# Loading and turning one tile of u earlier, and moving another load of u to a later hook, in a fused gated attention and feed-forward kernel

## The chip, the cores and the metric

The kernel runs on one core of a Trainium2 chip. The metric is the device time of one execution in microseconds (us). Times inside a profile are counted from the first instruction of the span.

## The reference

There are 8 batches of 3072 rows. `u` and `v` have 256 columns, `z` has 64. Attention is made from `z` alone, so the score matrix is symmetric, and there is no softmax:

```python
scores = scale * np.matmul(z, z.transpose(0, 2, 1))   # scale = 1 / 3072
attn = np.maximum(scores, 0.0) ** 2
x = u * np.matmul(attn, v)                            # 24576 rows of 256
h1, h2 = x @ w1, x @ w2                               # 256 -> 1024
out = np.maximum(h1, h2) @ w_out                      # 1024 -> 256
```

All inputs and the output are 32-bit floats.

## The kernel before

**Tiles.** The rows of a batch are 24 tiles of 128. Four tiles are a group (`G = 4`, 6 groups per batch), two groups a couple (3 per batch). The score matrix of a batch is handled in 4x4-tile blocks, `A[b, g, blk]`, kept in 28 slots of SBUF (class `Block`). Only blocks with `blk >= g` are computed; a block on the other side of the diagonal is the transpose of its partner, made by a DMA transpose from SBUF to SBUF (`mirror`, L273, the DMA issued at L275). A score pair (`score_pair`, L209) is two matmuls (L223) into two PSUM tiles `s_ps`, a ReLU on ScalarE (L236) and a square on VectorE (L244).

**Stages.** Groups 0 to 3 of batch 0 are done one by one (loop `for i in range(PLAIN)`, L617). For each, `attn_unit` (L286) multiplies the blocks with `v` into four accumulators, and the code between the matmuls issues scores ahead, loads, transposes and the gates. Here `i` is the group, `n` the tile of the step. The edges of a group run all its tiles for one half of the columns (`dc = 0`) and then for the other; what is hooked to a tile `n` is issued in the pass with `dc = 0`. After that come the couples, from couple 2 of batch 0 on (L758), each a list of steps of two matmuls each (L908). Couple 2 of batch 0 is a "plain" one (`PLAIN_COUPLES`, L46): it needs no sums of blocks prepared, and it works through the blocks 4 and 5 first (steps 0 to 31), then 0 and 1, then 2 and 3. All later couples form seven products from sums of blocks (a Strassen scheme). Before each couple stands a feed-forward stage for two earlier groups (`second`, L705, which calls `ff`, L448, twice). The first such stage, for groups 0 and 1 of batch 0, is the one at L753.

**u.** `load_u` (L189) allocates a tile `un` from a pool of two buffers and loads it by GpSimd-issued DMAs (L195), in two DMAs for groups above 1. With `held=True` a one-column memset on VectorE (L192) goes first, so that the DMA waits for the place of that memset in VectorE's order. `turn_u` (L197) transposes it by a DMA that SyncE issues (L199) into a tile `uT`, also from a pool of two. The gate (`gate`, L433; instruction L437 on VectorE, one per half of the columns) multiplies the attention result with `uT` into `xT`, the input of the feed-forward. With two buffers, the load of `u` of group 5 takes the buffer of group 3, and may start when the turn of group 3 has read it.

**Feed-forward.** `ff` first makes 8 tiles `d_ps` (L453) with a ReLU on ScalarE (L460) each, then two PSUM tiles `o_ps` (L467, L476) of two 128-row tiles each. A ScalarE copy (L488) moves each into a tile `o_sb` from a pool of three buffers, and a DMA on GpSimd's queue (L489) writes it out. `hook(1, nb)` is called after each of the 8 parts, `hook(2, t)` after the matmuls of row tile `t` and before the copy and the output that follow an odd `t`. `second` puts its list of tasks, one at a time, at the hooks (1, 0), (1, 3), (2, 0), (2, 1), (2, 2), (2, 3) of each `ff`:

```python
places = {(1, 0): 1, (1, 3): 1, (2, 0): 1, (2, 1): 1, (2, 2): 1, (2, 3): 1}
...
for _ in range(places.get((stage, n), 0)):
    if tasks:
        tasks.pop(0)()
```

The tasks come from `prepared` (L726), which for a plain couple returns the gates alone:

```python
if i in PLAIN_COUPLES:
    return {}, list(gates)
```

**z.** The transposed `z` of a batch is in three pieces of eight tiles, turned by `turn_z` (L147, DMA at L151 on SyncE's queue). Pieces of batch 1 are turned during group 2 (piece 0) and group 3 (pieces 1 and 2) of batch 0, since couple 2 of batch 0 computes scores of batch 1 between its steps. Its first scores on piece 1 stand at step 27, those on piece 2 at step 61.

**Order.** The program is laid out by hand (`tc.manual_schedule()`): each engine runs its instructions in the order in which the code issues them, and waits on semaphores where an instruction needs another engine's or a DMA's result, or a buffer that is still in use. SyncE's queue carries all DMA transposes (mirrors, u, z, and once w2, L673); GpSimd's queue carries the loads of u, v, z and the outputs. Around the change SyncE's order is: turn of u of group 2, transpose of w2, mirror (0,4), z piece 0, mirror (1,4) at tile 20 of group 2, mirrors (3,4) and (0,5) at tile 0 of group 3, turn of u of group 3 at tile 3, mirror (1,5), z piece 1, mirror (3,5), z piece 2, then the turns of u of groups 4 and 5. Mirror (g, blk) is the block of rows g and columns blk.

Of the kernel before, what the change touches and what calls it, by code (L numbers as in the profile page):

```python
# [11 lines left out]
def kernel(  # L12
# [55 lines left out]
    def by_tile(x):  # L68
        return x.rearrange("(p t) d -> p t d", t=NT)
# [34 lines left out]
    def load(tile_, source):  # L104
        dma = nc.gpsimd.dma_start(out=tile_, in_=source)  # L105
        if pace:
            tc.add_manual_dep(dma.ins, pace[-1].ins.name, AFTER, reason="paced")
# [23 lines left out]
    def zT_pe(lo, n, engine):  # L131
        tp = mm_psum.tile([P, n, P], bf16, name="tpz", tag="mm")
        for j in range(n):
            nc.tensor.transpose(
                tp[:, j, :], zd_first(lo + j, 1).rearrange("p t h d -> p (t h d)"), ident
            )
        copy = nc.scalar.copy if engine == "act" else nc.vector.tensor_copy
        for k in range(0, n, G):
            copy(zT[:, lo + k : lo + k + G, :], tp[:, k : k + G, :])
# [49 lines left out]
    def load_u(b, g, held=False):  # L189
        un[b, g] = unat.tile([P, G, D], bf16, name="un")  # L190
        if held:
            nc.vector.memset(un[b, g][:, 0, 0:1], 0.0)  # L192
        step = 2 if b or g > 1 else G
        for k in range(0, G, step):
            load(un[b, g][:, ds(k, step), :], by_tile(u[b])[:, ds(g * G + k, step), :])  # L195

    def turn_u(b, g):  # L197
        t = upool.tile([P, G, KD, P], bf16, name="uT")
        nc.sync.dma_start_transpose(  # L199
            t.rearrange("p a c r -> p (a c) r"), un[b, g].rearrange("p a d -> p (a d)")  # L200
        )
        uT[b, g] = t
# [70 lines left out]
    def mirror(b, g, blk):  # L273
        t = Block(turned=True)
        nc.sync.dma_start_transpose(  # L275
            t.ap.rearrange("p (k r) -> p k r", r=P), A[b, g, blk].ap
        )
        A[b, blk, g] = t
        A[b, g, blk].release(after=COOL)
# [6 lines left out]
    def attn_unit(b, g, t, acc, dc, first, last):  # L286
        blk, j = divmod(t, G)
        a = A[b, g, blk]
        for half in range(2):
            rows = ds(half * R, R)  # L290
            nc.tensor.matmul(  # L291
                a.out(acc[half, dc]),
                v_at(b, t, dc)[rows],
                a.moving(rows, j),
                start=first,
                stop=last,
            )
        if dc == KD - 1 and j == G - 1:
            a.release()
# [4 lines left out]
    def drain(acc, dcs, copy=nc.scalar.copy):  # L304
        hs = {}
        for dc in dcs:
            hs[dc] = new_h()
            copy(hs[dc], acc[1, dc])
        for dc in dcs:
            nc.vector.tensor_add(hs[dc], hs[dc], acc[0, dc])  # L310
        return hs

    def drain_fast(acc, dc):
        hs = [new_h() for half in range(2)]
        nc.scalar.copy(hs[1], acc[1, dc])
        nc.vector.tensor_copy(hs[0], acc[0, dc])
        return hs
# [205 lines left out]
    def emit_pair(wait=0):  # L523
        nonlocal done
        early = done < 12
        finish = score_pair(
            *pairs[done], dve_half=1 if early and done % 3 == 0 else None, halves=done == 0
        )
        done += 1
        if wait:  # L530
            due.append((tick + wait, finish))
        else:
            finish()
# [10 lines left out]
    def steps_of(i):  # L544
        tiles, both = range(NT), range(KD)
        head = edge(i - 1) if i else 0
        tail = NT - edge(i)
        steps = [(n, dc) for dc in both for n in tiles[:head]]
        steps += [(n, dc) for n in tiles[head:tail] for dc in both]
        return steps + [(n, dc) for dc in both for n in tiles[tail:]]  # L550

    def pair_slots(i):
        return (
            [1, 3] + list(range(6, 40, 4)),
            list(range(3, 41, 4)),
            list(range(3, 41, 4)),
            list(range(0, 44, 4)),
        )[i]

    def need(b, g, n):  # L560
        most = pair_at[b, g, 2 * g]
        for t in range(n + 1):
            if t // G >= g:
                most = max(most, pair_at[b, g, t // 2] + 1)
        return most

    with tc.manual_schedule():
# [18 lines left out]
        def new_acc():  # L586
            return {
                (half, dc): acc_tile(2 * half + dc) for half in range(2) for dc in range(KD)
            }
# [27 lines left out]
        for i in range(PLAIN):  # L617
            b, g = groups[i]
            if i:
                acc = new_acc()  # L620
            new, slots = {}, pair_slots(i)
            for slot, (n, dc) in enumerate(steps_of(i)):
                tick += 1
                k = need(b, g, n)
                upto = max(k, min(done + 1, k + AHEAD)) if slot in slots else k
                while done < min(upto, len(pairs)):
                    emit_pair()
                if i == 0 and slot in (10, 22):
                    zT_pe(12 if slot == 10 else 20, 8 if slot == 10 else 4, "act")
                    if slot == 22:  # L630
                        for x in z_first:
                            x.release()
                attn_unit(b, g, n, acc, dc, n == 0, n == NT - 1)
                if n == NT - 1 and i < PLAIN - 1:
                    if i < 2:
                        new[dc] = drain_fast(acc, dc)
                    else:
                        new.update(drain(acc, [dc]))
                if dc:
                    continue  # L640
                if i in (1, 2) and n in (5, 8):
                    k = n // 8
                    nc.vector.tensor_add(sums[k][0], *sums[k])
                    sums[k] = sums[k][0]
                first = 17 if i == 3 else 11
                if i and n == first:
                    gates = gate(*groups[i - 1], sums)
                if i and n in (first, first + 3):
                    gates.pop(0)()
                if i == 0 and n == 14:  # L650
                    turn_u(0, 0)
                if (i, n) in ((1, 8), (2, 1), (3, 1)):
                    load_u(0, i, held=True)
                if (i, n) == (3, 14):
                    load_u(0, 4, held=True)
                if i and n == (0, 16, 14, 3)[i]:
                    turn_u(0, i)
                if (i, n) in ((0, 18), (2, 12)):
                    w_in = ((w2_sb, moe_w2), (w1_sb, moe_w1)) if i == 0 else ((w_out_sb, moe_w_out),)
                    nc.vector.memset(w_in[0][0][:, 0, 0:1], 0.0)  # L660
                    for w_sb, w in w_in:
                        nc.gpsimd.dma_start(
                            out=w_sb, in_=w.rearrange("(c p) f -> p c f", p=P)
                        )
                if later and n % 4 == 0 and (i == 3 or i and n > 12):
                    later.sort(key=lambda block: block[2])
                    mirror(*later.pop(0))
                if i == 2 and n == 16:
                    nc.vector.tensor_sub(w15_sb, w1_sb, w2_sb)
                    w1.release()  # L670
                    w2.release(after=COOL)
                if (i, n) == (2, 15):
                    nc.sync.dma_start_transpose(  # L673
                        w2T.ap.rearrange("p (k r) -> p k r", r=P), w2.ap
                    )
                if (i, n) in ((1, 16), (2, 14)):
                    load_z(1, i - 1, held=True)
                if (i, n) in ((2, 17), (3, 4)):
                    turn_z(1, i - 2)
                if (i, n) == (3, 5):  # L680
                    load_z(1, 2, held=True)
                if (i, n) == (3, 17):
                    turn_z(1, 2)
            sums = new
# [41 lines left out]
        def prepared(i, gates):  # L726
# [25 lines left out]
        forms, tasks = prepared(PLAIN // 2, gate(b, g, sums))  # L752
        second(  # L753
            PLAIN // 2 - 2,
            [lambda: load_u(0, 5)] + tasks,
        )

        for i in range(PLAIN // 2, len(couples)):  # L758
# [177 lines left out]
            if i + 1 < len(couples):  # L936
                forms, tasks = prepared(i + 1, gates)
            else:
                tasks = gates
# [33 lines left out]
```

## Time and profile before

| | |
|---|---|
| median of 5 runs | 919.12 us (915.37 to 919.2) |
| the profiled execution | 918.5 us |
| its span, first to last instruction | 916.7 us |
| mean granted clock of TensorE | 0.996 |
| TensorE busy | 899.2 us, 98% of the span |
| VectorE busy | 722.3 us, 79% |
| ScalarE busy | 601.4 us, 66% |
| GpSimd busy | 161.0 us, 18% |
| DMA moved | 145.61 MB, mean 159 GB/s |

In the profile, PE is TensorE (PEld its weight loads), DVE is VectorE, ACT is ScalarE, POOL is GpSimd and SP is SyncE. A row of a timeline gives start, duration (both in us), engine, line of the kernel, instruction, output<-input and the number of instructions merged into the row; in brackets follow the idle time of the engine before it and what ended that. A q behind an engine's name stands for its instruction queue. A row of a table by stretches gives the stretch, its length, the busy time and number of instructions of each engine (TensorE, its weight loads, VectorE, ScalarE, GpSimd), the granted share of TensorE's clock, the mean busy share of the DMA engines (with overlaps counted, so it can pass 1), and GB/s. A row of the chain gives start, duration and what the end of the program was waiting for.

### The profile page before, as it was taken

The page shows a single profiled execution, that of the slowest core. Times are in us where ns is not written, and L with a number is a line of the kernel's source. Part 1 is how long each engine was busy: PE and PEld are TensorE (multiplying, and loading weights), DVE is VectorE, ACT ScalarE, POOL GpSimd, SP SyncE. Part 2 cuts the span into 40 slices and gives each one's busy share as a digit, 9 for nine tenths or more (in the row PEclk, how much of TensorE's full clock was granted, in tenths as well). Part 3 has the DMA queues.
Part 4 walks back from the last instruction along what each step waited for, and adds up shares of the span by engine and source line. Part 5 has one row for each costly group of instructions (what it writes and reads, how often), then busy time and mean ns, then how long its engine had stood idle before and what let it go on. Part 6 is the DMA issues. An engine that isn't in the chain of part 4 may idle for free.

```text
span 916.7 us, 19395 instructions
## 1 busy us (share of the span) xinstructions
PE 899.2 (98%) x7478; PEld 520.1 (57%) x7526; DVE 722.3 (79%) x1098; ACT 601.4 (66%) x1192; POOL 161.0 (18%) x303
## 2 busy tenths in 40 slices
PE   9996999999999999999999999999999999999998
PEld 4454465564655655656556656466465564655655
DVE  6743599788997799987998979979799788995640
ACT  7973966667676676666766676766666667673445
POOL 4111111212202122111212021130230212101000
PEclk9998999999999999999999999999999999999999
DMA  9999998999999897999969999799989989988201
GB/s 175 176 163 194 177 166 132 197 176 155 180 174 162 176 165 151 178 154 169 202 114 204 148 173 169 136 204 159 157 171 142 186 162 171 160 160 145 78 24 70
DMA packets 396557, 145.61 MB, mean 159 GB/s; under 512 B 361904, under 2 KB 387632, under 8 KB 396464
## 3 DMA queue, kind: packets, MB, share of 16 engines
q1 hardware_dynamic: 359040, 91.79, 65.0%
q0 software_dynamic: 37424, 52.58, 32.0%
q8 instruction: 59, 0.97, 0.5%
q14 instruction: 34, 0.28, 0.1%
HBM read 59.77 MB, written 25.17 MB: 93 GB/s over the span
## 4 chain that ended last, share of the span: by engine, by line
PE 94%; DMA 3%; DVE 1%; issue 1%; ACT 1%; SPq 0%; POOL 0%; ACTq 0%; POOLq 0%; DVEq 0%
PE acc L908 44%; PE o_ps L476 18%; PE d_ps L453 18%; PE s_ps L223 7%; PE o_ps L467 4%; PE acc L291 2%; DMA blk<-blk 1%; DMA out_dram<-o_sb 1%; ACT r_sb L236 1%; DMA un<-in_u_dram 1%; DVE blk L244 1%; DMA uT<-un 0%; PE acc L595 0%; PE w2o_ps L691 0%; SPq L275 0%
## 5 line engine op out<-in xcount | busy, mean ns | idle before, releaser
L908 PE MATMUL acc<-blk,v_sb 64*128 64x512 bf16 x2208 | 453.5, 378 | 0.0
L236 ACT ACTIVATE r_sb<-s_ps 128x512 bf16<-128x512 f32 (+3 forms) x672 | 335.4, 559 | 120.3 <-PE s_ps L223 76.1
L908 PE MATMUL acc<-blk,vt 64*128 64x512 bf16 x1512 | 364.1, 376 | 0.0
L908 PEld LDWEIGHTS <-v_sb 64*128 64x128 bf16 x2208 | 179.3, 94 | 142.4 <-issue 15.4
L244 DVE TENSOR_TENSOR blk<-r_sb 128x1024 bf16<-128x1024 bf16 x257 | 172.4, 688 | 88.2 <-ACT r_sb L236 82.7
L460 ACT ACTIVATE g_sb<-d_ps 128x512 bf16<-128x512 f32 x384 | 193.4, 626 | 29.4 <-PE acc L908 17.9
L476 PE MATMUL o_ps<-w_out_sb,g_sb 128*128 128x256 bf16 x1536 | 175.5, 273 | 0.0
L908 PEld LDWEIGHTS <-vt 64*128 64x128 bf16 x1512 | 139.2, 94 | 62.9
L453 PE MATMUL d_ps<-xT,w_sb 128*128 128x512 bf16 x720 | 167.7, 379 | 2.6 <-issue 0.2
L476 PEld LDWEIGHTS <-g_sb 128*128 128x128 bf16 x1536 | 150.3, 98 | 17.3
L488 ACT COPY o_sb<-o_ps 128x512 f32<-128x512 f32 (+1 forms) x98 | 56.4, 578 | 141.3 <-PE o_ps L476 131.7
L223 PE MATMUL s_ps<-zT 64*128 64x512 bf16 (+3 forms) x676 | 131.4, 358 | 7.7 <-ACT o_sb L488 7.4
L489 POOL DMA_DIRECT2D out_dram<-o_sb x88 | 48.2, 548 | 498.6 <-ACT o_sb L488 498.6
L785 DVE TENSOR_TENSOR h_sb<-h_sb,acc 128x512 f32<-128x512 f32 x168 | 109.4, 682 | 28.3 <-ACT h_sb L789 20.9
L453 PEld LDWEIGHTS <-w_sb 128*128 128x128 bf16 x768 | 73.3, 98 | 89.4 <-issue 9.8
L347 DVE TENSOR_TENSOR blk<-blk,blk 128x2048 bf16<-128x2048 bf16 x63 | 77.2, 1225 | 4.5 <-DMA blk<-blk 2.4
L343 DVE TENSOR_TENSOR blk<-blk,blk 128x2048 bf16<-128x2048 bf16 x63 | 76.7, 1218 | 0.0
L800 DVE TENSOR_TENSOR blk<-blk,blk 128x2048 bf16<-128x2048 bf16 x63 | 76.6, 1218 | 0.0
L351 DVE TENSOR_TENSOR blk<-blk,blk 128x2048 bf16<-128x2048 bf16 x63 | 73.3, 1219 | 3.3 <-DMA blk<-blk 3.3
L105 POOL DMA_DIRECT2D un<-in_u_dram x94 | 50.2, 549 | 124.5 <-DMA uT<-un 87.6
L437 DVE SCALAR_TENSOR_TENSOR xT<-h_sb,uT 128x512 bf16<-128x512 f32 x96 | 62.0, 684 | 6.3 <-DMA uT<-un 5.0
L242 DVE TENSOR_TENSOR blk<-r_sb 128x512 bf16<-128x512 bf16 (+3 forms) x162 | 46.2, 323 | 19.5 <-ACT r_sb L236 18.5
(49 smaller groups left out, 357.9 us busy)
## 6 DMA issues: line engine op xcount, KB each, us to landing
out_dram<-o_sb POOLq DMA_DIRECT2D x88, 256.0 KB, 3.8
un<-in_u_dram POOLq DMA_DIRECT2D x92, 128.0 KB, 5.2
v_sb<-in_v_dram POOLq DMA_DIRECT2D x74, 128.0 KB, 6.0
blk<-blk SPq DMA_TRANSPOSE x240, 5.0
v_sb<-in_v_dram POOLq DMA_DIRECT2D x11, 256.0 KB, 7.3
zn<-in_z_dram POOLq DMA_DIRECT2D x21, 128.0 KB, 4.7
out_dram<-o_sb SPq DMA_DIRECT2D x6, 256.0 KB, 2.0
blk<-in_moe_w_dram POOLq DMA_DIRECT2D x2, 512.0 KB, 7.6
```

The source lines that it names most:

```text
L223: nc.tensor.matmul(s_ps[h][:, lo[h] :], zT[rows, z_at(b, blk * G + tiles[h]), :], zT[rows, q + lo[h] // P : q + G, :].rearrange("p t c -> ...
L236: nc.scalar.activation(o, s, AF.Relu)
L244: nc.vector.tensor_mul(a[:, k : k + 2, :], r, r)
L343: nc.vector.tensor_add(*alike(f["S1"], f["A21"], f["A22"]))
L347: nc.vector.tensor_sub(*alike(f["S2"], f["S1"], f["A11"]))
L351: nc.vector.tensor_sub(*alike(f["S3"], f["A11"], f["A21"]))
L453: nc.tensor.matmul(d_ps, w15_sb[:, kc, ts(nb, P)], xT[:, kc, :], start=(kc == 0), stop=(kc == KD - 1),)
L460: nc.scalar.activation(g_sb[:, nb, :], d_ps, AF.Relu)
L476: nc.tensor.matmul(o_ps[t // 2][:, t % 2, :], g_sb[:, nb, ts(t, P)], w_out_sb[:, nb, :], start=False, stop=(nb == KF - 1 and t % 2 == 1),)
L785: nc.vector.tensor_add(out, a, b_)
L800: nc.vector.tensor_sub(f["A12"].ap, f["A12"].ap, f["S2"].ap)
L908: mm = nc.tensor.matmul(a.out(acc[name]), w()[rows], a.moving(rows, j), start=name not in opened, stop=left[name] == 0,)
```

## The change

`u` of group 3 was loaded at tile 1 of group 3 and turned at its tile 3. It is now loaded at tile 19 of group 2 (`i + n // 19` is 3 there) and turned at tile 22 of group 2. In the first feed-forward stage, the load of `u` of group 5 was the first of the tasks that the stage takes at its hooks; it is now put behind the first three tasks of the list, or behind all of them where there are fewer.

```diff
-                if (i, n) in ((1, 8), (2, 1), (3, 1)):
-                    load_u(0, i, held=True)
+                if (i, n) in ((1, 8), (2, 1), (2, 19)):
+                    load_u(0, i + n // 19, held=True)
                 if (i, n) == (3, 14):
                     load_u(0, 4, held=True)
-                if i and n == (0, 16, 14, 3)[i]:
+                if (i, n) == (2, 22):
+                    turn_u(0, 3)
+                if (i, n) in ((1, 16), (2, 14)):
                     turn_u(0, i)
...
         forms, tasks = prepared(PLAIN // 2, gate(b, g, sums))
         second(
             PLAIN // 2 - 2,
-            [lambda: load_u(0, 5)] + tasks,
+            tasks[:3] + [lambda: load_u(0, 5)] + tasks[3:],
         )
```

## The prediction, made before the changed kernel ran

> **What bounds the kernel now.** I first read busy shares and the slices: TensorE is busy 899.2 of 916.7 us, so only a TensorE hole can pay. The change touches u of groups 3 and 5, so I asked for the chain that ended last around the first ff stage (start, length, what; us):
>
> ```profile
> 71.94 3.42 PE d_ps L453 x15
> 75.36 1.54 SPq L275
> ...
> 77.06 3.25 DMA uT<-un
> ...
> 81.38 0.52 POOL un L105
> 81.91 6.25 DMA out_dram<-o_sb
> ...
> 88.26 0.59 ACT o_sb L488
> ```
>
> Here the chain leaves TensorE: turned u of group 3 lands at 77.06+3.25 = 80.31, then GpSimd loads u of group 5, then the first output goes out and lands at 88.16, then ScalarE copies. The timeline of TensorE gives the hole, and the stretches after it the clock:
>
> ```profile
> 81.16 0.38 PE L223 MATMUL s_ps<-zT 64*128 64x512 bf16 x1
> 88.89 0.58 PE L223 MATMUL s_ps<-zT 64*128 64x512 bf16 x1 [7.36 <-ACT o_sb L488]
> 88.90 2.28 PE L908 MATMUL acc<-blk,v_sb 64*128 64x512 bf16 x8
> 84.00:88.00 4.00, 0.00 (x0) 0.00 (x0) 0.00 (x0) 0.00 (x0) 0.00 (x0) 0.74 1.22 257
> 88.00:92.00 4.00, 3.10 (x16) 1.35 (x17) 1.39 (x2) 3.30 (x7) 0.55 (x1) 0.50 1.28 173
> ```
>
> TensorE stands 7.36 us, for ScalarE's copy of the fourth o_sb; pool o_sb has three buffers, so that copy waits for output 1 to land. The granted clock then is 0.50. It falls at 85.92 and is full again at 92.75, so 92.75 - 88.89 = 3.86 us of matmuls run at half speed and lose 1.93. The hole costs 7.36 + 1.93 = **9.29 us**. GpSimd's timeline says why output 1 was late:
>
> ```profile
> 63.74 1.06 POOL L105 DMA_DIRECT2D un<-in_u_dram  x2 [8.66 <-DVE un L192]
> 80.86 1.06 POOL L105 DMA_DIRECT2D un<-in_u_dram  x2 [16.06 <-DMA uT<-un]
> 81.91 1.64 POOL L489 DMA_DIRECT2D out_dram<-o_sb  x3
> ```
>
> Three outputs leave at once behind the load of u of group 5, although ScalarE had copied the first at 70.77. That load needs the buffer of u of group 3, so it waits 16.06 us for the turn. The turn is late because SyncE's queue runs far behind the code (the x3 issue at 66.71, 70.86 and 72.96):
>
> ```profile
> 64.92 1.68 SPq L151 DMA_TRANSPOSE zT<-zd  x1
> 66.71 10.18 SPq L275 DMA_TRANSPOSE blk<-blk  x3
> 77.06 1.23 SPq L199 DMA_TRANSPOSE uT<-un  x1
> 78.39 1.71 SPq L275 DMA_TRANSPOSE blk<-blk  x1
> 80.20 1.89 SPq L151 DMA_TRANSPOSE zT<-zd  x1
> ```
>
> [...] transposes move about 1000 packets per us alone (77 to 79), some 300 while loads and outputs run (82 to 91).
>
> **Part 1: u of group 3 earlier.** Load: one 59 ns VectorE memset and two GpSimd DMAs (0.53 us each) move from tile 1 of group 3 to tile 19 of group 2, from 50.56 to about 47.5. They stay behind the same z load and ahead of the next, so no queue order on GpSimd changes. The z load ahead of them lands at 53.65 and their packets come after its, so I count no gain and no loss. Were the zn load slowed by 1 us, VectorE's copies (waiting 2.17 us for it) would be 1 us later; pools r_sb and s_ps cover that, uncovered 1 us. The buffer is free (the turn of group 1 landed at 37.37), so the memset waits for nothing; it comes before L310, whose wait costs TensorE 0.44 us at 48.49: at most 0.06 more.
>
> Turn: one SyncE instruction of 1.23 us. Following the code, the line of mirrors there is (1,4) at 66.71 (tile 20 of group 2), (3,4) at 70.86, (0,5) at 72.96 (both tile 0 of group 3). The turn moves from behind (0,5) to behind (1,4), past two mirrors. It issues at 70.8 instead of 77.06, 6.3 us earlier; its inputs landed long before and its target is free since the gate of group 1 at 45.1. Mirror (1,4) lands at 72.62; 1024 packets more at about 800 per us, the rate there, is 1.3: **landing about 73.9** (it was 1.30 behind its predecessor in the trace too). Late bound: an instruction fetch of 1.6 us at 74.72 held transposes until 77.1; a turn caught by it lands near 77.
>
> **Part 2: u of group 5.** The list of tasks for this ff stage holds only the two gates of group 3, since couple 2 is a plain one and nothing else is prepared. So tasks[:3] is both gates, and the load becomes task three, run at the hook after tile t=0 of the o_ps part. The first output is written at t=1. **The load is thus still ahead of the first output on GpSimd's queue**; only the gates move up one place on VectorE, where nothing stands between. They run after the L310 adds end at 75.44 instead of 80.43, and nothing waits for them. Part 2 costs and brings 0.
>
> **What is late next.** GpSimd: landing 73.9, loads 0.55 later at 74.45, output 1 at 73.9 + 1.60 = 75.5 (offsets as in the trace: 80.31, 80.86, 81.91). Output 1 takes 6.25 us, as before behind the same two loads: lands at 81.75. The same fetch may hold it; I add 0.5, half of a delay of about 1 us. TensorE is unhurt when the copy starts by 80.8 (0.7 us from landing to matmul, needed at 81.4). So a hole of 82.25 - 80.75 = **1.5 us** stays (bounds 0, if the output lands in 5 us, and 4)[...].
>
> Next comes z. The scores of step 27 of couple 2 (TensorE at 96.19) need z transpose piece 1, issued at 80.20 and landed at 86.58: 9.6 us of slack. TensorE now comes there 9.29 - 1.5 = 7.8 earlier, at 88.4. SyncE's total up to that issue is the same, being a permutation, but loads and outputs now fall on 75 to 82 instead of 82 to 88 and take bandwidth from mirrors (0,5), (1,5) and this z. About 3000 packets fewer in that stretch are 3 us, of which the outputs' earlier end gives back about half: landing near 88 +/- 2. Mean hole **0.6 us** (bounds 0 and 3). Mirrors (0,5) and (1,5) are in front of it in the queue and needed only from step 32, at 89.5. Mirror (3,5), landing 92.38 before, is needed from step 68, near 99. The last v load landed at 118.33 for VectorE's use at 124.82; its issue is paced by TensorE, so 6.5 us of cover moves along. SyncE waits for new work at 126.19, so its backlog is gone there; from 92.75 to 881 no TensorE gap is above 0.08 us, so the shift should reach the end.
>
> **Sum.** 9.29 - 1.5 - 0.6 = 7.2 us. The profiled execution: span 916.7 to 909.5, with the 1.8 us around it 918.5 to 911.3. The median before, 919.12, is 0.6 above that execution: **911.9**.
>
> **Rivals.**
> A, the forecast: gain 5 to 8.5, time 910.6 to 914.1; chance 0.60.
> B, output 1 really escapes the wait, because it goes first or lands in under 5 us: no hole, only z to wait for, 9.29 - 0.3 = 9.0, time 910.1 (909.1 to 910.6). For: the description says outputs go first. Against: the task list is two long. 0.12.
> C, the turn is caught by the fetch or by mirrors' packets and lands at 77 or later: output at 78.6, landing 84.8, hole 4.1 with about 1 us of clock lost; gain 9.29 - 5.1 = 4.2, less 0.6 for z: 915.5 (914.1 to 916.3). For: that fetch stands 0.8 us behind the expected landing. 0.14.
> D, no difference: the wait moves whole to z piece 1, DMA being what bounds the stretch (DMA share 1.2 from 80 to 119); TensorE standing at step 27 until about 95: 918. Against: in 76 to 80 the share was 0.88, so there is room. 0.08.
> E, slower: the turn in front of mirrors (3,4) and (0,5), with outputs on their heels, delays z piece 1. Slower by 2.76 us means that after a gain of 7.8 step 27 stands 10.5 us, of which 1.9 is clock: z lands at 88.4 + 8.6 = 97.0, 10.4 later than before. At 98 the time is 922.9. The moved turn is 1.3 us of DMA time, so that needs a queue collapse that I don't see: 0.06.
>
> 0.3%, 2.76 us, is about what a measurement of this kernel can tell from no change. Faster: A + B + C = 0.86; within: D = 0.08; slower: E = 0.06. Range 909.2 to 916.0: A, nearly all of B, most of C, about 0.82. The low end is the whole 9.29 and the 0.63 wait for w2's transpose (64.74) gone too.
>
> **What would show it.** Right: GpSimd's 16.06 us wait shrinks to about 9 (64.8 to 74.45); output 1 leaves at 75 to 76, still behind both loads; the gap of 7.36 is under 2.5 and the clock stays full at 85; a small new wait for zT may stand near 88. Wrong: output ahead of the loads (B); turn landing after 77 (C); a long TensorE wait on zT or a mirror between 85 and 100 (D, E).

## The result, and the profile after

The changed kernel takes as long as the kernel before, or 0.1% longer: 918.67 us (median of 43 executions) against 917.52 us (80 executions of the kernel before on the same chips), a ratio of 1.0014 with a 95% interval of 1.0002 to 1.0025. I had forecast 911.9 us. Single executions spread from 914.0 to 928.8, those of before from 914.1 to 923.4, so one profile of either kernel is one draw. The ratios in this document leave out executions more than 1.5% above the fastest of the same kernel; where that leaves out many of them (7 of 22 in e4, 8 of 22 in e13), the median of all is given beside the ratio.

The profiled execution took 918.47 us. Its span is 915.5 us, 1.2 us shorter than before, but 3.0 us lie outside the span, where it was 1.8. The matmul of group 0 that waits for w2's memset starts 1.06 us later in it than in the profile of before (20.79 against 19.73), so times in this stretch compare after taking 1.06 off. The chain that ended last (start, duration, what; us):

```profile
71.89 3.35 DMA uT<-un
...
76.31 0.52 POOL un L105
76.84 9.18 DMA out_dram<-o_sb
86.12 0.59 ACT o_sb L488
```

The first output no longer waits for a late turn: it leaves at 76.84 instead of 81.91. But it needs 9.18 us to land, where it needed 6.25. The timelines of GpSimd and then of SyncE:

```profile
75.79 1.06 POOL L105 DMA_DIRECT2D un<-in_u_dram  x2 [10.13 <-DMA uT<-un]
76.84 1.11 POOL L489 DMA_DIRECT2D out_dram<-o_sb  x2
```

```profile
71.89 1.23 SPq L199 DMA_TRANSPOSE uT<-un  x1
73.29 13.31 SPq L275 DMA_TRANSPOSE blk<-blk  x3
86.70 1.31 SPq L151 DMA_TRANSPOSE zT<-zd  x1
```

Both loads of u of group 5 are still ahead of the first output. SyncE turns u of group 3 first, but the three mirrors behind it, (3,4), (0,5) and (1,5), take 13.31 us to issue, and z piece 1 is issued at 86.70 instead of 80.20 and lands at 91.64 instead of 86.58. TensorE's timeline, and then two stretches of time (columns as explained above):

```profile
86.75 0.58 PE L223 MATMUL s_ps<-zT 64*128 64x512 bf16 x1 [4.13 <-ACT o_sb L488]
```

```profile
84.00:88.00 4.00, 1.25 (x7) 0.49 (x8) 0.27 (x1) 1.88 (x4) 0.54 (x1) 0.72 1.10 269
88.00:92.00 4.00, 4.00 (x22) 1.75 (x20) 1.80 (x3) 2.51 (x6) 0.53 (x1) 0.50 1.18 249
```

The hole is 4.13 us long instead of 7.36. The clock is half from 85.73 to 92.56, so the restart loses (92.56 - 86.75) / 2 = 2.9 us instead of 1.93. In this draw the hole costs 7.0 us and not 9.29. Of these 2.3 us the start that is 1.06 us later takes nearly half, which leaves the 1.2 us by which the span is shorter.

### The profile page after: what moved, and what is told of

The parts are those of the page before. It is cut to its first block, busy times and chain, and to the rows that moved or that the text cites. A ratio compares the mean times of both kernels' runs of the same rounds, so it can differ in the third digit from the quotient of the medians.

```text
span 915.5 us, 19396 instructions
## 1 busy us (share of the span) xinstructions
PE 901.0 (98%) x7478; PEld 521.5 (57%) x7526; DVE 722.8 (79%) x1098; ACT 601.9 (66%) x1192; POOL 160.2 (18%) x303
## 4 chain that ended last, share of the span: by engine, by line
PE 95%; DMA 2%; ACT 1%; DVE 1%; issue 1%; SPq 0%; POOL 0%; ACTq 0%; DVEq 0%; POOLq 0%
PE acc L910 44%; PE d_ps L453 18%; PE o_ps L476 18%; PE s_ps L223 7%; PE o_ps L467 4%; PE acc L291 3%; DMA out_dram<-o_sb 1%; ACT r_sb L236 1%; DMA zT<-zd 1%; DVE blk L244 0%; DMA uT<-un 0%; PE acc L595 0%; PE tpz L134 0%; DVE w_sb L671 0%; DVE xT L437 0%
```

## The experiments

The experiments set two theories against each other: H, the loss is the hole behind the fourth output copy, and the rest of the stretch has slack; M, the DMA engines have so much to do between 60 and 130 us that a wait taken away in one place comes back in another. Each run has a label, as e2; the text in front of its result is what was expected before it ran.

### Part 2 alone (e2)

```diff
-            [lambda: load_u(0, 5)] + tasks,
+            tasks[:3] + [lambda: load_u(0, 5)] + tasks[3:],
```

> The kernel before with part 2 alone (the load of u of group 5 behind the tasks). My working says that part 2 leaves GpSimd's order as it was, so all theories expect a ratio of 1.000 +/- 0.002, GpSimd issuing both loads of u of group 5 ahead of the first output after a wait of about 16 us, and TensorE's gap of about 7 us for the fourth output copy. If part 2 did something of its own, the order of loads and outputs in the trace would differ from before. The run also gives a second profiled execution of what should be the same program as before, and so shows how much the gap varies.

Ratio 1.0007 (0.9989 to 1.0025). The instruction lists of all five engines are, in their order, those of the kernel before; those of part 1 alone are likewise those of the whole change. Part 2 does nothing. The profiled execution of what is the same program as before has a hole of 5.56 us and half speed from 82.66 to 89.49: 5.56 + (89.49 - 86.10) / 2 = 7.3 us. The 9.29 I counted was one draw of a varying loss.

### The outputs really first (e3)

```diff
-            tasks[:3] + [lambda: load_u(0, 5)] + tasks[3:],
+            tasks + [lambda: None] * 4 + [lambda: load_u(0, 5)],
```

> The changed kernel, with the load of u of group 5 put at the first hook of the second ff, so that it really stands behind outputs 1 and 2. Theory H (the loss is the hole behind the fourth output copy, the rest of the stretch has slack): outputs 1 and 2 leave at about 72 and 74, output 1 lands before 80, no gap at the fourth copy, ratio 0.990 to 0.993. Theory M (DMA work bounds the stretch, the wait only moves): a new wait of TensorE of 4 us or more on z piece 1 (step 27 of couple 2) or on a mirror between 85 and 100, ratio 0.996 to 1.001.

Ratio 1.0008 (0.9988 to 1.0029). Outputs 1 and 2 leave at 71.59 and 73.34, the first lands at 76.05, and the hole at the copy is gone. TensorE now waits for z:

```profile
91.22 0.61 PE L223 MATMUL s_ps<-zT 64*128 64x512 bf16 x2 [3.75 <-DMA zT<-zd]
```

That is M's wait, a little under the 4 us it named. H falls: with the outputs really first, nothing is gained.

### The hole taken away without moving a DMA (e4, e5)

```diff
-                o_sb = opool.tile([P, 2, D], fp32, name="o_sb")
+                if (b, g, t) == (0, 1, 3):
+                    o_sb = new_h().rearrange("p (t d) -> p t d", d=D)
+                else:
+                    o_sb = opool.tile([P, 2, D], fp32, name="o_sb")
```

In the kernel before:

> The kernel before, with the fourth output copy of the first ff stage writing to a free buffer of another pool, so that it waits for no output; no DMA and no order changes. H: the gap of 7.4 us and the half-speed stretch after it go, ratio 0.990 to 0.992 (about 9 us). M: the gap turns into a wait for z piece 1, which landed at 86.6 and would be needed at 86.9, or for a mirror; ratio 0.996 to 1.001.

In the changed kernel:

> The changed kernel with the same spare buffer for the fourth output copy. H: same gain as the kernel before with it, ratio 0.990 to 0.993. M: outputs and loads that leave at 76 instead of 81 hold z piece 1 back (it landed at 91.6 in the changed kernel's profile), so TensorE waits for it some 3 to 5 us at step 27 of couple 2: ratio 0.995 to 1.000, and slower than the kernel before with the spare buffer.

Kernel before: 1.0001 (0.9978 to 1.0024), with executions from 908.4 to 928.5; the median of all 22 is 920.98, against 917.42 without the spare buffer. Changed kernel: 1.0068 (1.0044 to 1.0093). TensorE's row with the wait, first of the kernel before with the spare buffer, then of the changed one:

```profile
104.67 0.61 PE L223 MATMUL s_ps<-zT 64*128 64x512 bf16 x2 [7.60 <-DMA zT<-zd]
```

```profile
99.68 0.61 PE L223 MATMUL s_ps<-zT 64*128 64x512 bf16 x2 [12.39 <-DMA zT<-zd]
```

The waits for z are as long as the hole was, or longer. M had the wait right, and understated e5 (it said 3 to 5 us and 0.995 to 1.000), where the late piece is z piece 1. In e4 the late piece is z piece 2, issued at 87.41 and landing only at 104.62, after 17.21 us; in the kernel before it took 5.84 us and landed at 94.07. GpSimd's timeline of e4 shows what is beside it:

```profile
84.86 0.54 POOL L105 DMA_DIRECT2D v_sb<-in_v_dram  x1 [1.25 <-PE s_ps L223]
88.10 0.54 POOL L105 DMA_DIRECT2D v_sb<-in_v_dram  x1 [2.70 <-PE acc L911]
91.33 0.53 POOL L105 DMA_DIRECT2D v_sb<-in_v_dram  x1 [2.70 <-PE acc L911]
94.57 0.53 POOL L105 DMA_DIRECT2D v_sb<-in_v_dram  x1 [2.71 <-PE acc L911]
```

The v loads of batch 1 are paced by TensorE. In the kernel before the first of them left at 93.39, after the hole and 0.7 us before z piece 2 landed. A TensorE that doesn't stop calls for them 8.5 us earlier, and all four of these left before that piece landed.

### v and u of group 5 later (e6, e7, e8, e9)

These four ask whether the v loads are what holds z back (M1 below) or not (M2). e6 is e4 with this, e9 the kernel before with this alone:

```diff
-                    *((14 + 12 * k, load_v, 1, (1, 2, 0)[k // 2], k % 2 * G, G) for k in range(6)),
+                    *((34 + 12 * k, load_v, 1, (1, 2, 0)[k // 2], k % 2 * G, G) for k in range(6)),
```

e7 is the kernel before with this, e8 has both:

```diff
-            [lambda: load_u(0, 5)] + tasks,
+            tasks,
...
-                    (1, turn_u, 0, 4),
-                    (4, turn_u, 0, 5),
+                    (36, load_u, 0, 5),
+                    (50, turn_u, 0, 4),
+                    (66, turn_u, 0, 5),
```

> The kernel before with the spare buffer for the fourth output copy, and the six loads of v of batch 1 at steps 34, 46, ... 94 of couple 2 instead of 14, 26, ... 74. Theory M1 (without the hole, the v loads, which TensorE's progress paces, come among the late transposes and hold the z pieces back): the z piece that landed at 104.6 now lands before 97, no TensorE wait over 1 us between 80 and 115, ratio 0.989 to 0.993. Theory M2 (the line of transposes, outputs and u is late by itself, v or not): a wait for z of 4 us or more stays, ratio 0.997 to 1.002.

> The kernel before with the load of u of group 5 at step 36 of couple 2 and the turns of u of groups 4 and 5 at steps 50 and 66 (before: first ff stage, steps 1 and 4). Nothing stands in front of the outputs, which leave when copied; there is no spare buffer. v stays at steps 14 to 74. M1: no hole at the fourth copy, but z is still held back by v, by less than with the spare buffer, since the u load and two turns (some 4 us of DMA time) are out of the way: a z wait of 1 to 5 us, ratio 0.993 to 0.999. M2: z in time, ratio 0.990 to 0.992.

> Both: u of group 5 and the turns of groups 4 and 5 late, and v at steps 34 to 94. M1: neither hole nor z wait over 1 us, ratio 0.989 to 0.991, and runs close to each other (spread under 4 us). M2: as with u late alone. If v or u are then too late for the end of couple 2, a new wait of TensorE stands between 108 and 125.

> The kernel before with v at steps 34 to 94 and nothing else. The hole at the fourth copy is there before any v load is issued, so both theories expect it to stay: ratio 0.998 to 1.001. A gain of over 0.5% would say that v was in the way even with the hole.

| kernel | ratio, 95% interval | waits of TensorE in its profile |
|---|---|---|
| e6: spare buffer, v late | 0.9948 (0.9921 to 0.9975) | 2.91 at 140.01, 0.97 at 125.80 |
| e7: u of group 5 late | 0.9995 (0.9975 to 1.0015) | 2.73 at 89.43, for z |
| e8: both late | 1.0043 (1.0022 to 1.0064) | 5.10 at 125.61, 3.97 at 131.89 |
| e9: v late alone | 0.9995 (0.9981 to 1.0008) | 10.41 at 91.74, the hole |

e6 says that v was what held z back in e4 (M1): z piece 2 now takes 6.66 us and lands at 92.93, and ten of its 22 executions lie between 908 and 911, what I had forecast for the change or a little better. The other twelve lie between 913 and 929, so the ratio misses M1's range by a little (the median of all 22 is 914.35, against 917.55). Its two waits are for VectorE, which waits for mirrors there. e9 shows that v late alone is worth nothing while the hole stands. e7 came out a little above M1's figures, with the z wait that M1 named. e8 went wrong as its last sentence feared: VectorE waits up to 7.56 us for the turn of u of group 5, which lands at 122.88, its adds for couple 3 come late, and TensorE waits for those.

### Between the two (e12, e13)

e12 is e4 with v at steps 26 to 86. e13 also holds the mirrors of batch 1 other than (1,0,1) back:

```diff
-        return b == 0 or (g + blk) % 2
+        return b == 0 or (g + blk) % 2 and (not held_back or (b, g, blk) == (1, 0, 1))
...
+            held_back[:] = [True][: i < 3]
```

> The kernel before with the spare buffer and v at steps 26, 38, ... 86 (8 steps earlier than in the run with v at 34, where half of the executions were near 908 to 911 and the others lost up to 20 us). If those lost it to v arriving late for the sums of couple 3, v at 26 gives a lower median, ratio 0.990 to 0.994; if they lost it to z, which v at 26 meets sooner, it is worse, 0.996 to 1.000.

> As with v at 26, and the mirrors of batch 1 other than (1,0,1) wait for the end of couple 2 (three or four transposes of 2 us less between 100 and 112, where u, v and they met). M: the DMA engines have that much less to do before couple 3, most executions near 908 to 911, ratio 0.989 to 0.993. If these mirrors come back as waits in couple 3 or 4, ratio 0.997 or more with a TensorE gap between 125 and 190.

e12: 1.0027 (1.0006 to 1.0047), worse than both figures; nothing waits for z in its profile, but this does, at the start of couple 3:

```profile
132.76 0.58 PE L911 MATMUL acc<-blk,vt 64*128 64x512 bf16 x1 [7.14 <-DVE blk L351]
```

VectorE's subtraction there had itself waited 7.15 us for a DMA transpose that landed at 131.45, the last of a line of mirrors that landed 4 to 6 us apart (117.12, 122.88, 126.72, 131.45). I read this as a third place at which the same backlog comes out. e13: 1.0013 (0.9988 to 1.0037), and the median of all 22 is 922.05, against 917.59, so putting mirrors off gained nothing; four of its 22 executions are at 909 to 914, the rest at 919.7 to 928.1. Its profiled execution is one of the long ones (924.09); in it TensorE stands 11.29 us at 137.52, behind the same subtraction as in e12. That is the return in couple 3 which its text named as the other outcome, but one long execution does not settle why e13 is no better than e12.

### DMA work taken out (e10, e14, e15)

```diff
     def mirror(b, g, blk):
+        if (b, g, blk) in ((0, 3, 4), (0, 0, 5)):
+            A[b, blk, g] = A[b, g, blk]
+            return
```

These three kernels leave out the transposes of two mirrors, though the result needs them; every matmul, copy and load stays. It is done in the changed kernel (e10), in e6 (e14) and in e5 (e15):

> The changed kernel without the transposes of mirrors (3,4) and (0,5): their blocks are used unturned, so part of batch 0's output is wrong, while every matmul, copy and load stays. It takes some 4 us of DMA time out from between the turn of u of group 3 and the first outputs. Theory M (DMA work bounds the stretch): output 1, which took 9.2 us to land, lands in 6 us or less, the hole of 4.1 us falls under 2 us, z piece 1 lands 4 us or more earlier, ratio 0.991 to 0.996. If the landing time is the output's own and not that of the transposes beside it, the hole stays and the ratio is 0.999 to 1.002.

> The kernel before with the spare buffer and v at steps 34 to 94, and without the transposes of mirrors (3,4) and (0,5), whose blocks are used unturned, so part of batch 0's output is wrong. If the sum of DMA work from 60 to 130 is the bound (M), 4 us less of it lets nearly all executions run at 906 to 911 with no TensorE wait over 1 us between 60 and 150: ratio 0.988 to 0.992. If the slower half of the executions with v at 34 had another cause, half of them stay over 913.

> The changed kernel with the spare buffer (ratio 1.007, TensorE waiting 12.4 us for z piece 1) without the transposes of mirrors (3,4) and (0,5), which stand ahead of that z piece in SyncE's line; part of batch 0's output is wrong. M: z piece 1 comes 5 us or more earlier, the wait falls by 6 us or more, ratio 0.992 to 0.999. If z was late for another reason, the ratio stays over 1.004.

| kernel | ratio with both mirrors | ratio without them |
|---|---|---|
| changed kernel | 1.0014 (1.0002 to 1.0025) | 0.9948 (0.9927 to 0.9969) |
| before, spare buffer, v late | 0.9953 (0.9923 to 0.9982) | 0.9912 (0.9883 to 0.9940) |
| changed, spare buffer | 1.0068 (1.0044 to 1.0093) | 0.9917 (0.9886 to 0.9948) |

All three gain, by 3.8 to 13.9 us for two transposes that the matmuls never waited for by name; the intervals of the second pair overlap. e14's six executions lie between 908.6 and 913.1, where nine of 18 of the same kernel with the mirrors (e16) lie above that: with some 4 us less of DMA work the slow half is not seen, though six executions are few. The 4 us are an estimate from the profile of before: 1825 and 1910 transpose packets moved from the issue of each of the two mirrors (70.86 and 72.96) to the next issue, and transposes alone do about 1000 per us. Six of e15's seven lie between 909.1 and 913.3. The seventh, 922.33, is the profiled one: nothing waits for z in it, but TensorE stands at the third place again:

```profile
136.65 0.58 PE L916 MATMUL acc<-blk,vt 64*128 64x512 bf16 x1 [9.87 <-DVE blk L354]
```

In e10 output 1 lands in 7.40 us and TensorE's gap is 2.27; I had named 6 and under 2. While output 1 is on its way, 1759 transposed packets move in e10, 2346 in the changed kernel and 1788 in the kernel before, where it took 6.25 us; so the transposes beside it are part of the delay, and the rest is not explained. z piece 1 lands at 81.75, not 91.64. It is also issued at 73.72 instead of 86.70, as SyncE's line is shorter by two mirrors. These runs therefore don't tell less DMA work from an earlier place in that line; z piece 1 ahead of the mirrors, with nothing left out, was not tried. That DMA work counts by itself is seen in e6, where SyncE's order is that of e4 and z piece 2 takes 6.66 us instead of 17.21. The chain of e10 has the row

```profile
75.17 7.40 DMA out_dram<-o_sb
```

### The changed kernel again, and the early turn alone (e11, e16, e17)

e11 is the changed kernel, e16 is e6 once more, and e17 is e16 with the change in it.

> The changed kernel itself, for a second profiled execution. Under M the hole of the fourth copy varies with how loads, outputs and transposes share the DMA engines: a hole between 2 and 8 us, the early turn of u of group 3 landing 2 to 5 us after its issue near 71 and the first output 6 us or more after its own. If the hole is 4.1 us again within 0.3, the time is fixed by something else.

> The kernel before with the spare buffer and v at 34 to 94, once more, beside the others of this call: ratio 0.993 to 0.997 as before (0.9948), with executions from 908 to over 920. It is the version to hand on if it holds.

> The changed kernel with the spare buffer and v at 34 to 94: what the early turn of u of group 3 is worth once the hole is gone and v is out of the way. M: the turn and the outputs behind it go in front of mirrors and z piece 1 in a stretch that has no DMA time to spare, so no gain over the same kernel without the change and probably a loss: ratio 0.994 to 1.003, with a z wait at step 27.

e11 (919.05 us): the turn lands 3.2 us after its issue at 72.03, output 1 takes 8.57 us, the hole is 3.31, and two other waits stand beside it: 1.49 for the transpose of w2 (0.63 in the kernel before) and 2.03 at 144.86 for VectorE (none before). e16 holds: 0.9953 (0.9923 to 0.9982), a median of 914.32; in its profiled execution, span 908.5, TensorE has no wait over 0.1 us between 60 and 150. e17: 0.9984 (0.9963 to 1.0004), a median of 916.26, with a z wait at step 27:

```profile
90.70 0.60 PE L223 MATMUL s_ps<-zT 64*128 64x512 bf16 x2 [3.71 <-DMA zT<-zd]
```

Where the hole is gone and v is out of the way, the kernel with the early turn of u of group 3 came out 0.3% slower (0.9984 against 0.9953). The intervals overlap, so a loss is likely and not shown.

## Why the prediction was wrong

**Its reading of the hole was right.** TensorE's stop was the fourth copy waiting for output 1, output 1 waited behind the load of u of group 5, and that for the turn. e4 removes the stop by a buffer alone.

**Part 2 was right.** It does nothing; the lists of instructions and e2 show it.

**Part 1's times were right.** With 1.06 taken off, the turn issues at 70.8 (forecast 70.8), lands at 74.2 (73.9), and output 1 leaves at 75.8 (75.5).

**"Output 1 takes 6.25 us, as before behind the same two loads" failed.** It took 9.18, and 8.57 in e11. The loads were the same, the company was not: before, the mirrors in front of z piece 1 had been issued by the time the output left; after, three of them ran beside it. e10 takes two of these out and gets 7.40, so 1.8 of the 2.9 us went with them. The stop of 1.5 us that I left became 4.13. That is the length which rival C gave, but C's path was another: there the turn landed at 77 or later.

**"The clock stays full at 85" failed.** It fell at 85.73. This was about the stop of 1.5 us, and the stop of 4.13 us lost 2.9 us of clock; but that the shorter stop would lose none was my estimate, shown by no trace: in e10 one of 2.27 us still had a half-speed stretch of 3.4 us, from 83.15 to 86.56.

**"Mean hole 0.6" for z rests on the same error.** I added up SyncE's issues and took the DMA engines as having room. With 1.06 taken off, z piece 1 was issued 5.4 us later than before and landed at 90.6, outside the 88 +/- 2. That z stayed hidden in the changed kernel is because TensorE itself was late. Where it isn't (e5), z costs 12.39 us.

**The step behind both is the weight given to rival D.** It said that the wait moves to z, DMA being the bound, and I gave it 0.08 because the DMA share between 76 and 80 was 0.88. Taken apart, that stretch has one us in which hardly anything moved, a share of 0.06 (last section), and three with a share of 1.15, as in the rest of the stretch:

```profile
76.00:77.00 1.00, 1.00 (x11) 0.90 (x10) 0.00 (x0) 0.44 (x1) 0.00 (x0) 1.00 0.06 6
77.00:80.00 3.00, 3.00 (x29) 2.39 (x29) 0.00 (x0) 0.59 (x1) 0.00 (x0) 1.00 1.15 243
```

The time came out at D's 918, but in the changed kernel that is luck: what is left there is the hole, and not D's wait for z, which stands in e3, e5 and e17. I also counted the waits of TensorE after 92.75, saw none, and concluded that the rest has slack. The absence of waits behind a hole says only that the hole was long enough. A sum over the whole stretch could have been made from the profile of before. The DMA queues in three stretches of it (packets, MB, share of 16 engines): 76.9 to 79.9, where transposes are alone; 100 to 110, with v loads; and 61 to 130:

```profile
q1 hardware_dynamic: 2824, 0.71, 111.9%
```

```profile
q1 hardware_dynamic: 2135, 0.53, 67.7%
q0 software_dynamic: 446, 0.82, 61.5%
```

```profile
q1 hardware_dynamic: 35318, 8.88, 84.6%
q0 software_dynamic: 1922, 3.67, 31.5%
```

Transposes (q1) alone do about 1000 packets per us (2824 in the 2.8 us that aren't idle). In the second stretch 2135 of them are 2.1 us, so the other 7.9 us are for 0.82 MB of v: about 0.1 MB per us, or a little more, since hardly anything moved in 1.3 of them. In the third, 35318 packets are 35 us; of the 3.67 MB, 2.1 MB are loads of u and v, 20 us, and 1.6 MB are six outputs. Between 82 and 88, 0.85 MB went beside 1627 transposed packets; 1.6 us for these and 2.6 for the 0.26 MB of u leave 1.8 us for 0.59 MB of outputs, so 1.6 MB are about 5 us. The estimate is 35 + 20 + 5 = 60 us of DMA work, in 69 us. Without the 9.3 us of the hole the stretch would be 59.7 us long. By this estimate, the hole was time that the DMA engines needed. The same sum over 130 to 200, where TensorE has no wait over 0.1 us, gives about 57 us in 70, so there is room there. This sum is an estimate from a few rows, and it takes the three kinds to add up; that 4 us less of it gives back 6.1, 3.8 and 13.9 us in e10, e14 and e15 is the evidence, with the limit on SyncE's line named there. e15 can gain more than the DMA time taken out: e5's profile loses 12.39 us to its wait for z and 3.0 to the half clock behind it, which lasts to 105.70, and e15's profile has no wait for z.

**The baseline was one draw.** I worked from a hole of 9.29 us; the same program had 7.3 in e2, and the median of 80 executions is 917.52, not 919.12.

**What stays open.** Why the changed kernel's executions reach further up (928.8) than those of before isn't shown by its two profiles, neither of which is one of the long ones; e5, e8, e12 and e15 show only that such lengths can come from waits for z or for couple 3.

## What to carry to other kernels

Before pricing a hole, add up the DMA time of the whole stretch around it, by kind: here that sum, an estimated 60 us, was near the length of the stretch less the hole, 59.7, and removing the hole alone gained nothing (e4: 1.0001). Moving one transfer moved what was behind it as well: with the turn issued 6.2 us earlier (1.06 taken off), output 1 left 6.1 us earlier and z piece 1 was issued 5.4 us later. Nor is the old duration to be taken along when the neighbours change: that of output 1 went from 6.25 us to 9.18. What paid here was to take the false wait away (a spare buffer) and at the same time put off loads that TensorE's own progress calls for: 0.9948 and 0.9953 in two measurements, better than both kernels.

## What the runs showed of the hardware

The half-speed stretches named above are 3.41 us long in e10 (83.15 to 86.56) and 6.83 in the profiles of before (85.92 to 92.75), of the changed kernel (85.73 to 92.56) and of e2 (82.66 to 89.49). The length of a stop did not decide alone whether there was one: the clock halved around stops of 2.27 us (e10), 3.31 (e11) and 3.71 (e17), and not around those of 2.73 (e7) and 2.91 (e6). In e10 TensorE started again at 83.31 and lost (86.56 - 83.31) / 2 = 1.6 us of clock. What tells the two kinds of stop apart isn't shown.

In the profile of before, a packet of 16 KB on the instruction queue (q8), the fetch of the prediction, took 1.63 us from 74.72 on. Of the transpose packets that started from 75.06 to 75.34, 15 took 1.77 to 2.06 us, where the median of all is 0.02; none started between 75.35 and 76.33, and only 31 from 75.30 to 77.05. In that profile 638 of the 690 transpose packets that took over 1 us start within 1 us of one of the 59 such fetches, which is a fifth of the time; 26 of the fetches came with fewer than five such packets. The two came together; that the fetch held the transposes isn't shown.
